# Value products of a head in two groups of three key tiles instead of three groups of two, beside the cluster work of the next pair

## The chip, the core and the metric

The kernel runs on one core of one Trainium2 chip. The metric is the device time of one execution in microseconds (us). The core's engines are TensorE (PE in the profile; PEld is its loading of weights), VectorE (DVE), ScalarE (ACT), GpSimd (POOL) and SyncE (SP), which here only issues DMAs.

## What is computed

The program chains three parts: an attention whose mask joins queries and keys of one cluster, a layer that mixes tokens, and two feed-forward networks. The change lies in the attention, for which the reference is, cut to what matters:

```python
batch, n_heads, seq, head_dim = (2, 8, 768, 64);  n_clusters = 16
q_assign = np.argmax(np.einsum('bhsd,hcd->bhsc', q_n, c_n), axis=-1)     # normalised q, centroids
k_assign = np.argmax(np.einsum('bhsd,hcd->bhsc', k_n, c_n), axis=-1)
mask = q_assign[:, :, :, None] == k_assign[:, :, None, :]
scores = scale * np.matmul(q, k.transpose(0, 1, 3, 2))
scores = np.where(mask, scores, -1000000000.0)
attn = exp(scores - max);  attn = attn / (np.sum(attn, axis=-1, keepdims=True) + 1e-09)
return np.matmul(attn, v).astype(np.float32)
```

Its output, 2 x 768 x 512, goes through h = x @ U @ V over the tokens, added to x, then relu(u @ w_ch1) @ w_ch2 added to u, then a gated network with a convolution over the tokens.

## The kernel before

All work of the attention runs in one loop of steps. There are 16 heads (two batches of eight), taken in eight pairs, and 6 query tiles of 128 rows per head, so 96 steps n; s = n mod 12 is the step in its pair, and r = (n - 7) mod 6 the place in the plan for the value products of head g, which run seven steps behind. The order is written by hand: each engine works through its own row of instructions in the order in which the function step() issues them (a manual schedule), and waits only for data or for a tile to be free.

What step n issues on PE, in this order:

- s_mm(n + 2): the scores of query tile n + 2 against all 768 keys, in four products. L349 (sc<-ab) brings the numbers, L360 (sc<-cd) a second part that also carries, in 16 rows of cd, the one-hot of the cluster, which is the mask. The tile of PSUM (ps_s) that they fill has two copies.
- if the table asks for it, onehot_t (L256): six transposes of the next pair's one-hot; from these ScalarE makes the tile os (onehot_rows, L262), which four DMAs of SP bring into the rows of cd (L270).
- the value products pv_mm (L403) of the key tiles that PLAN names for r: for one key tile k two products side by side, weights v, moving the transposed exponentials of all six query tiles of the head. The result stands in the PSUM tile pv (one copy) over all six key tiles.
- fin_t (L419): three transposes of a head's finished sum, after ScalarE has copied it out (fin_a, L412). Or, in some steps, a product of the token mixing of the batch that is done (L644, L664, L666).
- in step s = 0 sims_wide (L210): similarities to the centroids for the next pair but in the first; in step s = 2 sims_turn (L224), their transposes.
- t_mm(n) (L387): six transposes of the exponentials of step n, in two PSUM tiles of three (tr).

The other engines in step n: ScalarE and VectorE each copy one half of the transposes of step n - 1 out (t_out, L394); ScalarE computes the exponentials of step n + 1 (s_exp, L378); VectorE the row minimum of the negated scores of step n + 2 (s_max, L366). VectorE scales a finished head (fin_x: L425 reciprocals, L428 x<-at) and makes the one-hot of the next pair in five operations, L241 to L249, at the steps of ONEHOT_AT. Small tiles (tr, at, simw, sim, oht, and the mixing's) share three PSUM tiles, ps_t. In odd steps a weight word of later stages is made ready (L456 on ScalarE, L464 and L469 on VectorE).

PLAN has one entry for heads 0 to 14 and one for head 15: a table from r to key tiles, and the r at whose step fin_a follows. ROWS_AT is the step of onehot_t, first for pairs from the second on, then for the first pair. ONEHOT_AT holds the steps of the five operations, likewise.

Of the kernel before, what the change touches and what calls it, by code (L numbers as in the profile page):

```python
# [33 lines left out]
def tile_kernel(ctx: ExitStack, tc: tile.TileContext, qk, vv, cen, u_w, v_w, w1, w2, win, wout, conv, out):  # L34
# [4 lines left out]
    NT = S // P  # L39
# [340 lines left out]
    NK = NT // 2  # L380
# [325 lines left out]
            pump()  # L706


    PLAN = ({2 * k: (2 * k, 2 * k + 1) for k in range(NK)}, NT - 2), ({k: (2 * k, 2 * k + 1) for k in range(NK)}, NK - 1)
    MIX_AT = (2, 4, 8, 10)  # L710

    RAW_AT, V_AT = (5, 8), (8, 10)
    SIM_AT, TURN_AT, ONEHOT_AT, ROWS_AT = 0, (2, 2), ((2, 3, 3, 4, 4), (2, 3, 4, 5, 6)), (6, 7)

    def step(n):
        pair, s = divmod(n, 2 * NT)
# [18 lines left out]
        g, r = divmod(n - NT - 1, NT)  # L735
        ks, last = PLAN[g == NHEAD - 1]
        if 0 <= g < NHEAD:
# [513 lines left out]
```

## Time and profile before

| | |
|---|---|
| device time, median of 3 runs | 648.49 us (648.18 to 649.43) |
| the profiled execution | 649.08 us, of which its span is 647.3 us |
| attention stage | until about 244 us of the span |
| PE busy over the span | 637.2 us, 98% |
| VectorE, ScalarE, GpSimd busy | 430.7 (67%), 368.9 (57%), 304.8 us (47%) |
| TensorE clock granted | full in the whole span |

A busy PE need not be at its peak: products overlap, and what counts is the time from one start to the next. In the timeline below each row gives the start, the length, the engine, the line, what is written from what, the shapes and the number of instructions in a row; in brackets stands the idle time before and who ended it. PE's products of values appear as twice as many instructions as the program writes (x8 for a group of two key tiles).

### The profile page before, as it was taken

How to read it: one execution, taken by the hardware profiler on the slowest of the kernel's cores; microseconds unless marked ns; L12 is line 12 of the kernel's file. 1: busy time of each engine (PE TensorE's matmuls, PEld its weight loads, DVE VectorE, ACT ScalarE, POOL GpSimd, SP SyncE). 2: the span in 40 equal slices, each digit the busy share in tenths (PEclk: the TensorE clock that was granted, in tenths of full speed). 3: DMA queues.
4: the chain of work that ended last, by engine and by line, in shares of the span. 5: the costliest groups of instructions: out<-in, count | busy, mean ns of one | idle time of the engine just before them, and what ended most of it. 6: DMA issues, size and time to landing. Idle time of an engine off the chain costs nothing.

```text
span 647.3 us, 10456 instructions
## 1 busy us (share of the span) xinstructions
PE 637.2 (98%) x3850; PEld 545.7 (84%) x3850; DVE 430.7 (67%) x841; ACT 368.9 (57%) x749; POOL 304.8 (47%) x308
## 2 busy tenths in 40 slices
PE   8999999999999999999999999999999999999997
PEld 5767676666777766999899999999999998889986
DVE  6878787786868785496576666666656468641762
ACT  5867676767767764745554434343354488654730
POOL 3744444256544721913967454554346455413330
PEclk9999999999999999999999999999999999999999
DMA  7495676737353321102333232222212211200022
GB/s 187 102 237 125 130 165 123 169 72 180 64 128 74 91 66 33 34 1 66 104 124 100 66 97 66 66 66 65 66 33 69 95 33 61 71 1 1 1 99 97
DMA packets 17860, 55.50 MB, mean 86 GB/s; under 512 B 3120, under 2 KB 3760, under 8 KB 17808
## 3 DMA queue, kind: packets, MB, share of 16 engines
q1 hardware_dynamic: 14208, 40.08, 21.4%
q0 software_dynamic: 3600, 14.75, 11.5%
q8 instruction: 30, 0.49, 0.3%
q14 instruction: 22, 0.18, 0.1%
HBM read 50.19 MB, written 3.15 MB: 82 GB/s over the span
## 4 chain that ended last, share of the span: by engine, by line
PE 45%; DVE 4%; ACT 3%; POOL 1%; issue 1%; DVEq 0%; POOLq 0%
PE po L970 8%; PE acc L887 6%; PE acc L886 6%; PE acc L888 6%; PE pd L826 4%; PE pb L826 4%; PE pa L826 4%; DVE cv L941 2%; PE g L919 2%; PE g L920 2%; PE g L918 2%; PE pc L826 2%; DVE h L947 1%; ACT cv L937 1%; POOL wl L569 0%
## 5 line engine op out<-in xcount | busy, mean ns | idle before, releaser
L366 DVE TENSOR_SCALAR_CACHE_REDUCE e<-sc 128x768 f32<-128x768 f32 x96 | 91.6, 955 | 14.7 <-PE sc L360 13.2
L890 DVE TENSOR_TENSOR xa<-acc,xa 128x384 f32<-128x384 f32 x128 | 70.1, 554 | 37.4 <-PE acc L888 37.4
L378 ACT ACTIVATE e<-sc,nb 128x768 f32<-128x768 f32 x96 | 87.0, 906 | 7.9 <-DVE e L366 7.4
L886 PE MATMUL acc<-r,vh 128*128 128x384 f32 x256 | 86.3, 337 | 0.1
L887 PE MATMUL acc<-r,vh 128*128 128x384 f32 x256 | 85.7, 335 | 0.3 <-POOL r L869 0.3
L387 PEld LDWEIGHTS tr<-identf,e 128*128 128x128 f32 x576 | 64.6, 140 | 25.2 <-issue 6.8
L888 PE MATMUL acc<-r,vl 128*128 128x384 f32 x256 | 85.6, 334 | 0.0
L387 PE MATMUL tr<-identf,e 128*128 128x128 f32 x576 | 81.7, 277 | 0.3 <-DVE pt L394 0.2
L403 PE MATMUL pv<-pt,rv 128*64 128x384 f32 x384 | 72.6, 499 | 0.0
L394 ACT COPY pt<-tr 128x384 f32<-128x384 f32 x96 | 45.9, 479 | 42.5 <-PE tr L387 42.4
L394 DVE COPY pt<-tr 128x384 f32<-128x384 f32 x96 | 53.2, 554 | 23.4 <-PE tr L387 22.1
L595 POOL TENSOR_TENSOR vl<-wx,vh 128x512 fp32r<-128x512 f32 x24 | 30.8, 1297 | 61.1 <-ACT vh L594 61.1
L349 PE MATMUL sc<-ab 128*128 128x384 f32 x192 | 57.5, 380 | 0.9 <-ACT e L378 0.6
L941 DVE SCALAR_TENSOR_TENSOR cv<-h,cw,cv 128x383 f32<-128x383 f32 (+1 forms) x64 | 38.2, 620 | 25.8 <-ACT cv L937 24.7
L360 PE MATMUL sc<-cd 80*128 80x384 f32 x192 | 49.5, 340 | 0.1
L886 PEld LDWEIGHTS acc<-r,vh 128*128 128x128 f32 x256 | 48.0, 188 | 1.7 <-DVE xa L890 0.8
L887 PEld LDWEIGHTS acc<-r,vh 128*128 128x128 f32 x256 | 48.1, 188 | 0.6 <-POOL r L869 0.6
L888 PEld LDWEIGHTS acc<-r,vl 128*128 128x128 f32 x256 | 48.1, 188 | 0.0
L403 PEld LDWEIGHTS pv<-pt,rv 128*64 128x64 f32 x384 | 23.4, 136 | 28.8 <-issue 28.3
L869 POOL TENSOR_TENSOR r<-q,r 128x384 fp32r<-128x384 f32 x16 | 16.3, 1016 | 58.7 <-ACT r L868 55.2
L469 DVE SCALAR_TENSOR_TENSOR wx<-wb,wy 128x512 int32<-128x512 int32 (+1 forms) x42 | 28.0, 667 | 21.8 <-POOL vl L595 11.0
L569 POOL TENSOR_TENSOR wl<-wx,wh 128x512 fp32r<-128x512 f32 (+1 forms) x32 | 36.4, 1153 | 10.4 <-ACT wh L568 5.2
(241 smaller groups left out, 1527.2 us busy)
## 6 DMA issues: line engine op xcount, KB each, us to landing
raw<-in_w_dram SPq DMA_DIRECT2D x32, 512.0 KB, 3.8
cd<-in_qk_dram POOLq DMA_DIRECT2D x15, 384.0 KB, 4.5
ab<-in_qk_dram POOLq DMA_DIRECT2D x15, 384.0 KB, 5.6
raw<-in_win_dram SPq DMA_DIRECT2D x8, 512.0 KB, 3.8
raw<-in_wout_dram SPq DMA_DIRECT2D x8, 512.0 KB, 3.7
rv<-in_vv_dram SPq DMA_DIRECT2D x8, 384.0 KB, 4.5
out_dram<-xa SPq DMA_DIRECT2D x12, 256.0 KB, 2.0
ab<-in_qk_dram POOLq DMA_DIRECT2D x15, 192.0 KB, 5.8
```

The source lines that it names most:

```text
L349: nc.tensor.matmul(ps[:, f, 0:HS], ab[:, 0, c0:c0 + P], ab[:, 1, f * HS:(f + 1) * HS], start=True, stop=False)
L366: nc.vector.tensor_scalar(out=e, in0=ps[:, :, 0:HS], scalar1=-SCALE, scalar2=3e38, op0=ALU.mult, op1=ALU.min, accum_out=nb,)
L378: nc.scalar.activation(e, ps[:, :, 0:HS], AF.Exp, scale=SCALE, bias=nb, accum_out=st["sum", n // NT][:, n % NT:n % NT + 1])
L387: nc.tensor.transpose(pt[:, k, :], e[:, i, k * P:(k + 1) * P], identf)
L394: (nc.scalar.copy if i == 0 else nc.vector.tensor_copy)(to, st.pop(("t", n, i)))
L403: nc.tensor.matmul(acc[i * D:(i + 1) * D], vts[b, h // 2][:, h % 2, k], pt[:, k, i * NK:(i + 1) * NK].rearrange("p a b -> p (a b)"), start ...
L826: nc.tensor.matmul(o, l[:, k, w], r[:, k], start=first and not more, stop=last, skip_group_check=more)
L886: nc.tensor.matmul(acc, wh[:, f, ds_], r[:, 0], start=f == 0, stop=False)
L887: nc.tensor.matmul(acc, wh[:, f, ds_], r[:, 1], start=False, stop=False)
L888: nc.tensor.matmul(acc, wl[:, f, ds_], r[:, 0], start=False, stop=f == 1)
L890: nc.vector.tensor_add(o, acc, o)
L970: nc.tensor.matmul(po, g[:, ts], w[:, f], start=n == 0, stop=n == 6 * len(cs) - 1)
```

## The change

Three tables change, nothing else:

```diff
-    PLAN = ({2 * k: (2 * k, 2 * k + 1) for k in range(NK)}, NT - 2), ({k: (2 * k, 2 * k + 1) for k in range(NK)}, NK - 1)
+    PLAN = ({2: (0, 1, 2), 5: (3, 4, 5)}, NT - 1), ({k: (2 * k, 2 * k + 1) for k in range(NK)}, NK - 1)
...
-    SIM_AT, TURN_AT, ONEHOT_AT, ROWS_AT = 0, (2, 2), ((2, 3, 3, 4, 4), (2, 3, 4, 5, 6)), (6, 7)
+    SIM_AT, TURN_AT, ONEHOT_AT, ROWS_AT = 0, (2, 2), ((2, 2, 3, 3, 4), (2, 3, 4, 5, 6)), (6, 8)
```

For heads 0 to 14 the value products ran at r = 0, 2 and 4, two key tiles each, which are the odd steps of a pair; now they run at r = 2 and 5, three key tiles each, in steps s = 0, 3, 6 and 9. fin_a follows in the step of the last group (r = 5 instead of 4), and fin_t stays at the next r = 0, one step behind it instead of two. Head 15 keeps its plan. In the pairs from the second on, two of VectorE's five operations of the one-hot go one step ahead (step 3 to 2, 4 to 3); the first pair's transposes of the one-hot go from step 7 to step 8.

On PE, from step 10 of one pair to step 0 of the next (the third and fourth pair), there stands before (of the products L210 one row is shown):

```order
L349 MATMUL sc<-ab 128x384 x2
L360 MATMUL sc<-cd 128x384 x2
L387 MATMUL tr<-identf,e 128x128 x6
L349 MATMUL sc<-ab 128x384 x2
L360 MATMUL sc<-cd 128x384 x2
L403 MATMUL pv<-pt,rv 64x384 x4
L387 MATMUL tr<-identf,e 128x128 x6
L349 MATMUL sc<-ab 128x384 x2
L360 MATMUL sc<-cd 128x384 x2
L210 MATMUL simw<-rq,cbq 32x384
```

and in the changed kernel:

```order
L349 MATMUL sc<-ab 128x384 x2
L360 MATMUL sc<-cd 128x384 x2
L387 MATMUL tr<-identf,e 128x128 x6
L349 MATMUL sc<-ab 128x384 x2
L360 MATMUL sc<-cd 128x384 x2
L387 MATMUL tr<-identf,e 128x128 x6
L349 MATMUL sc<-ab 128x384 x2
L360 MATMUL sc<-cd 128x384 x2
L403 MATMUL pv<-pt,rv 64x384 x6
L210 MATMUL simw<-rq,cbq 32x384
```

The group has moved from step 11 to step 0, grown by two products, and stands directly ahead of the similarities; steps 10 and 11 hold scores and transposes alone. In the same way steps 4 and 5 do, ahead of step 6, where the one-hot's transposes are followed by a group.

On PE at the end of the stage, from the scores of the last query tile to the first product of the next stage (L826), before:

```order
L360 MATMUL sc<-cd 128x384 x2
L403 MATMUL pv<-pt,rv 64x384 x4
L387 MATMUL tr<-identf,e 128x128 x12
L403 MATMUL pv<-pt,rv 64x384 x4
L387 MATMUL tr<-identf,e 128x128 x6
L826 MATMUL pa<-u_2734,wh 128x384
```

and in the changed kernel:

```order
L360 MATMUL sc<-cd 128x384 x2
L403 MATMUL pv<-pt,rv 64x384 x6
L387 MATMUL tr<-identf,e 128x128 x18
L403 MATMUL pv<-pt,rv 64x384 x6
L826 MATMUL pa<-u_2732,wh 128x384
```

The transposes of the last three steps now stand in one row, and the last group of head 14 has moved from between them to behind them.

On ScalarE in the first pair, around the rows made of the one-hot (L262), before:

```order
L378 ACTIVATE e,sum<-sc,nb 128x768
L262 ACTIVATE os<-oht,ohs 64x768
L456 ACTIVATE wb<-raw 128x192
L394 COPY pt<-tr 128x3x128
L378 ACTIVATE e,sum<-sc,nb 128x768
```

and in the changed kernel:

```order
L378 ACTIVATE e,sum<-sc,nb 128x768
L456 ACTIVATE wb<-raw 128x192
L394 COPY pt<-tr 128x3x128
L378 ACTIVATE e,sum<-sc,nb 128x768
L262 ACTIVATE os<-oht,ohs 64x768
```

L262 has moved behind one more copy and one more exponential.

## Rows read from the trace of the kernel before

**Rows 1.** Waits of PE, 60 to 230 us: total us, how often, longest.

```profile
PE tr L387 <- DVE pt L394: 0.2, 1, 0.2
```

**Rows 2.** Timeline of PE, third pair, steps 1 to 5.

```profile
72.42 0.59 PE L349 MATMUL sc<-ab 128*128 128x384 f32 x2
...
77.38 0.59 PE L349 MATMUL sc<-ab 128*128 128x384 f32 x2
...
78.25 1.51 PE L403 MATMUL pv<-pt,rv 128*64 128x384 f32 x8
79.70 0.88 PE L387 MATMUL tr<-identf,e 128*128 128x128 f32 x6
80.33 0.59 PE L349 MATMUL sc<-ab 128*128 128x384 f32 x2
...
81.71 0.62 PE L349 MATMUL sc<-ab 128*128 128x384 f32 x2
```

**Rows 3.** Timeline, all engines: bare steps at the start, then a step at 108.82.

```profile
25.04 0.62 PE L349 MATMUL sc<-ab 128*128 128x384 f32 x2
...
25.80 0.90 ACT L378 ACTIVATE e<-sc,nb 128x768 f32<-128x768 f32 x1 [0.45 <-DVE e L366]
...
26.84 0.61 PE L349 MATMUL sc<-ab 128*128 128x384 f32 x2 [0.17 <-ACT e L378]
...
28.45 0.62 PE L349 MATMUL sc<-ab 128*128 128x384 f32 x2
...
108.82 0.59 PE L349 MATMUL sc<-ab 128*128 128x384 f32 x2
...
110.95 0.90 ACT L378 ACTIVATE e<-sc,nb 128x768 f32<-128x768 f32 x1 [0.34 <-DVE e L366]
```

**Rows 4.** Timeline of PE inside the group of rows 2, two narrow windows.

```profile
78.63 0.81 PE L403 MATMUL pv<-pt,rv 128*64 128x384 f32 x4
...
78.95 0.82 PE L403 MATMUL pv<-pt,rv 128*64 128x384 f32 x4
```

**Rows 5.** Timeline of PE, third pair, step 0.

```profile
70.13 0.59 PE L349 MATMUL sc<-ab 128*128 128x384 f32 x2
...
71.00 0.51 PE L210 MATMUL simw<-rq,cbq 128*32 128x384 f32 x1
...
71.78 0.87 PE L387 MATMUL tr<-identf,e 128*128 128x128 f32 x6
```

**Rows 6.** Timeline of PE, one-hot's transposes: first pair step 7, second pair step 6.

```profile
30.25 0.47 PE L256 MATMUL oht<-identb,oh 128*64 128x128 bf16 x5 [0.83 <-DVE oh L249]
...
32.00 0.88 PE L387 MATMUL tr<-identf,e 128*128 128x128 f32 x6
...
56.20 0.59 PE L349 MATMUL sc<-ab 128*128 128x384 f32 x2
...
58.15 0.59 PE L349 MATMUL sc<-ab 128*128 128x384 f32 x2
```

**Rows 7.** Timeline of VectorE, fourth pair, steps 1 and 2.

```profile
102.86 0.19 DVE L425 RECIPROCAL rs<-sum 128x6 f32<-128x6 f32 x1
103.81 0.56 DVE L428 TENSOR_TENSOR x<-at,rs 128x384 f32<-128x384 f32 x1 [0.77 <-PE at L419]
104.46 0.56 DVE L394 COPY pt<-tr 128x384 f32<-128x384 f32 x1
```

**Rows 8.** First pair: timeline, then DMA issues (KB each, us to landing).

```profile
31.88 2.40 SPq L270 DMA_DIRECT2D cd<-os  x4
...
37.67 0.30 PEld L360 LDWEIGHTS sc<-cd 80*128 80x128 f32 x2 [0.41 <-issue]
...
cd<-os SPq DMA_DIRECT2D x4, 48.0 KB, 4.9
```

**Rows 9.** Timeline at the end of the stage.

```profile
243.09 0.47 ACT L394 COPY pt<-tr 128x384 f32<-128x384 f32 x1
...
244.34 0.59 PE L826 MATMUL pa<-u,wh 128*128 128x384 f32 x2
```

## The prediction

> **What bounds the kernel now.** I read the waits of TensorE (PE) first. In the steady part of the attention stage, 60 to 230 us, PE waits for another engine once, 0.2 us in all [rows 1]: there the stage lasts as long as PE's own row of instructions. So an instruction or a switch of tile that is taken from PE is a gain in full, but only while nobody else becomes late, and the second question is how much room the other engines have. The timeline of PE gives what a step costs, from one first similarity product to the next (a is that moment below). A plain step (scores, six transposes) takes 81.71 - 80.33 = 1.38 us; a step with a group of two key tiles takes 80.33 - 77.38 = 2.95, so such a group costs 1.57 [rows 2]. Two neighbours with such a group, a head's closing transposes (fin_t) and the turn of the similarities take 77.38 - 72.42 = 4.96, so fin_t and the turn cost 4.96 - 2.95 - 1.38 = 0.63, about half each [rows 2].
>
> The room is seen in a loop through three engines. Scores have two PSUM tiles. From a to the exponential that reads the scores is 110.95 - 108.82 = 2.13 (VectorE's row minimum lies between them), and from the start of the exponential to the next scores into the same tile 26.84 - 25.80 = 1.04 [rows 3]. So step n+2 cannot begin sooner than 3.17 us after step n. Two plain steps are 2.76 of PE's work, a plain one and one with a group 4.33. Before the change every second step holds a group, so the loop is never seen after the first group. Ahead of it, in the bare steps at the start, it is: the starts 25.04, 26.84 and 28.45 are 1.80 and 1.61 apart instead of 1.38, and PE waits for the exponential by name [rows 3].
>
> **The change, what it saves.** Heads 0 to 14 get two groups of six products in place of three of four. In the trace a group of two key tiles is eight instructions in four starts of two side by side; the second and third stand at 78.63 and 78.95, so a start is 0.32 and a key tile 0.64 [rows 4]. A group of three tiles then costs 1.57 + 0.64 = 2.21. Per head 3 x 1.57 - 2 x 2.21 = 0.29, over 15 heads **4.35**.
>
> The similarities of the next pair come right behind a group, in six pairs. Alone they cost 72.42 - 70.13 - 1.38 = 0.91 [rows 2, 5]; behind a group they cost the way from the group's last start to their first, X, then 71.78 - 71.00 = 0.78 from their first to the transposes [rows 5], less the way Y from the group's last start to the transposes, which they cut off. Y is 79.70 - 78.95 - 0.32 = 0.43 [rows 2, 4]. X is not in the trace. Its ends are a start inside a group, 0.32, and Y, the way to products that use the array in another cut, as the similarities' do. I take that end, the nearer row: 0.91 - 0.78 = 0.13, times six **0.8** (with X = 0.32, 0.24 and 1.4). The Trainium skill, in TensorEngine Tiling (Array Packing), Key Properties, says that a change of the tiling mode drains the engine; products of values have 64 columns and similarities 32, so by that rule X is at the dear end and the sum stays 0.8; the rows around groups agree with it, none shows this pair.
>
> The one-hot's transposes stand ahead of a group in six pairs. Alone they cost 58.15 - 56.20 - 1.38 = 0.57; ahead of a group they stood once already, in the first pair, where the two took 32.00 - 30.25 = 1.75 to the transposes against 79.70 - 78.25 = 1.45 for a group alone [rows 2, 6]. So 0.27 is saved six times and lost once, since the first pair's now stand apart: **1.35**. Sum of the gains 6.5 us.
>
> **What it costs.** Plain steps now come in twos between the groups: steps 1 and 2, 4 and 5, 7 and 8, 10 and 11 of a pair.
> (1) Steps 4-5 and 10-11 hold nothing else, except where the token mixing fills them, from step 8 of the fifth pair to step 8 of the seventh. That leaves five places at 4-5 and four at 10-11 in which 2.76 us of work meets the loop's 3.17: 9 x 0.4 = **3.6**. The wait stands at the next step's scores, and on PE the group stands behind those: it cannot be worked off meanwhile. The Trainium skill, TensorE: Matmul & The Clock Gate, Part 3, The mechanism, says that products start strictly in program order, only weight loads go ahead; by that rule, too, the group waits, and it speaks against this change; the waiting starts of rows 3 agree.
> (2) Steps 7-8 hold fin_t (2.76 + 0.32 = 3.08 against 3.17): 0.1. Steps 1-2 hold fin_t and the turn (3.39), and here another wait ends last: VectorE, after the minimum of the scores (done by about 2.1 behind a), does the reciprocals, 0.19, the scaled output x that reads fin_t's tile, 0.56, and only then its half of the transposes, 0.56 [rows 7]: 3.4, while PE wants that PSUM tile (there are three) for the second half of the next transposes 3.39 - 0.3 = 3.1 behind a. Between 0 and 0.3, I take 0.2. Before, the group in the step behind gave the cover. Seven places 7-8 with 0.1, six at 1-2 with 0.2 and the last pair (no turn) with 0.1 are 2.0. In three or so of them a weight word on VectorE or the mixing's copy on ScalarE stands ahead of the copy that frees the tile as well, some 0.35 each: **3.0** together (1.0 to 4.5).
> (3) The first pair. Its one-hot's transposes go from step 7 to step 8, and the rows built from them (L262) follow about 1.7 us later, so the four DMAs that bring them to the scores' operand, issued at 31.88, are issued at some 33.6. They took 4.9 us to land, behind loads, and PE waited for them: its weight load waited 0.41 before 37.67 [rows 8]. In the new order PE is there about 0.75 sooner (a group of 1.57 and a wait of 0.83 for the one-hot [rows 6] are gone from step 7, 0.64 and 0.27 are added, and some 0.7 goes to the loop and to the tile that the late rows hold). If the DMAs land when they did, since the loads in front of them set that, PE waits 0.75 more; if they land all of the 1.7 later, 2.4; if they are 0.5 sooner, 0.3. I take 0.75, because the landing time is far over what 48 KB need and the loads are not moved. Steps 10-11 of this pair add 0.35: **1.1** (0.3 to 2.5).
> (4) The end. Before, a group stood between the last transposes but one and the last, and covered the last exponential and ScalarE's copy at 243.09 that frees a PSUM tile for them. That cover moves behind them: the last transposes begin no sooner than 243.09 + 0.47, 243.6, or, if the tile holds up their second half alone, 0.3 sooner; from their start to the next row is 0.63 [rows 2], then comes the group of three tiles, 1.45 + 0.64 from its first product to what follows it [rows 2, 4], and only then the product for the next stage that began at 244.34 [rows 9]: 246.0 to 246.3, 1.7 to 2.0 later. Of this 0.64 is the third key tile, in the sum already, which leaves 1.0 to 1.35: **1.2** (0.6 to 1.4 as bounds).
>
> Sum of the costs 3.6 + 3.0 + 1.1 + 1.2 = 8.9, less 6.5 is +2.4. The profiled execution took 649.08 (span 647.30), which becomes 651.5; it lies 0.6 above the median of the runs, 648.49, so the forecast is 648.49 + 2.4 = **650.9**. The later stages have the same instructions, and nothing moves there.
>
> The parts of the one-hot on VectorE that go one step sooner (two of five) stand in step 2 and 3 instead of 3 and 4. They have the whole step 4 and 5 as cover until the transposes in step 6; I price them at nothing, and at up to 0.3 in step 2, inside (2), where that cover is not the point: the copy behind them is.
>
> **Rivals.** *The waits cancel the gains* (same). The loop may be shorter where the minimum is not behind another operation, say 3.0: then (1) is 9 x 0.25, (2) near 2, and with (3) and (4) the costs are 6.5, the gains' own size: 648 to 649.5. Against it stands 3.17 from two separate rows and the early steps, which are no faster.
> *The groups' switches are the larger thing* (faster). Point from which it decides: the waits in the twos of plain steps are below 0.15 each, since VectorE and ScalarE, which a long group leaves idle, take each minimum and exponential up sooner than in rows 3, and the loop shrinks below 2.9. Then (1) is 1.3, (2) 0.8, (3) and (4) 2.0: 4.1 against 6.5 or 7, 645.6 to 646.5. For it: a step with a group gives the loop 4.33 - 3.17 = 1.2 us of slack to catch up in. Against it: both parts of the loop in rows 3 begin with the engine free, so nothing in them is a queue that could go.
> *A queue builds up* (much slower). ScalarE gets the copy out of the group's tile (L412) and that of the similarities (L215), each as large as the copy of 0.47 in rows 9, in the same step 0, and VectorE the one-hot's parts in step 2; where this ends after the next exponential is due, each of six pairs loses another 0.5 twice: + 6, 655.
> *It does not do what it says:* the order as built shows two groups per head and the similarities and one-hot's transposes beside them, so I leave this no chance of its own.
>
> **How the numbers follow.** Slower by the waits as summed (649.8 to 653) 0.50; a queue beside it, 0.10; cancelled 0.25; faster 0.15. What a measurement of this kernel can tell from no change is about 0.2%, 1.3 us: faster is below 647.2, slower above 649.8. That gives 0.15, 0.25 and 0.60. The range takes the forecast and the cancelling case, the bounds of (2) to (4), and part of the two ends: 646.9 to 653.8. The forecast's own range is 649.3 to 653.
>
> **What would show it.** In the profile after: PE waits for the exponential (L349 <- L378) about nine times 0.4 at starts of steps 0 and 6; transposes wait for VectorE's x or copy in steps 2 and 8; a pair of heads (twelve steps) takes longer, not shorter; groups cost 2.2 over a plain step; PE's busy time falls by about 6 while the span does not. It is wrong if two plain steps in a row take 2.8 us (the loop has room then), if twelve steps become shorter by about 0.8 (the gains of two heads and of the neighbours in full), or if the first product after the attention stage comes sooner than before.

## The result and the profile after

The changed kernel takes 652.71 us (median of 6 runs, 652.08 to 653.09) beside 649.38 of the kernel before on the same chip: a ratio of 1.0051, 95% interval 1.0040 to 1.0061. That is 3.3 us slower, 2.6 to 4.0; 2.4 were forecast, with 646.9 to 653.8 as the range. The profiled execution's span is 650.7 us, 3.4 more than before, so the profile shows the whole of it.

The row of the page with the engines' busy time, changed kernel:

```profile
PE 636.8 (98%) x3850; PEld 549.8 (84%) x3850; DVE 427.2 (66%) x841; ACT 368.3 (57%) x749; POOL 305.5 (47%) x308
```

PE works 0.4 us less than before, over a span 3.4 longer. Its waits in the attention stage, 40 to 250 us (total us, how often, longest):

```profile
PE sc L349 <- ACT e L378: 1.5, 8, 0.2
PE simw L210 <- DMA rk<-in_qk_dram: 0.8, 1, 0.8
PE tr L387 <- ACT pt L394: 0.4, 1, 0.4
PE tr L387 <- ACT e L378: 0.3, 1, 0.3
PE tr L387 <- DVE pt L394: 0.3, 1, 0.3
PE tr L387 <- ACT xa L672: 0.2, 1, 0.2
```

Before, there was the one wait of [rows 1]. These totals understate what is lost: step 5 below is 0.41 longer than a plain step, while the wait at its end has 0.17. The starts tell it. The timeline of PE, third pair, from step 0 on (which answers to [rows 2, 5 and 6]; each row of L349 is the start of a step, those left out among them being step 2 at 76.57 and step 8 at 90.89):

```profile
70.47 0.62 PE L349 MATMUL sc<-ab 128*128 128x384 f32 x2 [0.18 <-ACT e L378]
...
71.38 2.16 PE L403 MATMUL pv<-pt,rv 128*64 128x384 f32 x12
73.46 0.51 PE L210 MATMUL simw<-rq,cbq 128*32 128x384 f32 x1
...
74.25 0.87 PE L387 MATMUL tr<-identf,e 128*128 128x128 f32 x6
74.88 0.59 PE L349 MATMUL sc<-ab 128*128 128x384 f32 x2
...
78.50 0.59 PE L349 MATMUL sc<-ab 128*128 128x384 f32 x2
...
82.10 0.60 PE L349 MATMUL sc<-ab 128*128 128x384 f32 x2
...
83.48 0.61 PE L349 MATMUL sc<-ab 128*128 128x384 f32 x2
...
85.27 0.62 PE L349 MATMUL sc<-ab 128*128 128x384 f32 x2 [0.17 <-ACT e L378]
...
86.18 0.47 PE L256 MATMUL oht<-identb,oh 128*64 128x128 bf16 x5
...
88.57 0.87 PE L387 MATMUL tr<-identf,e 128*128 128x128 f32 x6
89.20 0.59 PE L349 MATMUL sc<-ab 128*128 128x384 f32 x2
...
92.36 0.60 PE L349 MATMUL sc<-ab 128*128 128x384 f32 x2
```

A reader should see three things. The loop: 85.27 - 82.10 = 3.17 us for two bare steps, to the hundredth what [rows 3] gave, and the scores at 85.27 name the exponential; step 5 takes 1.79 instead of 1.38 (step 4, at 1.38, is not longer). The group: step 3 takes 82.10 - 78.50 = 3.60, so a group of three tiles costs 2.22 over a plain step. The neighbours: step 0 is 74.88 - 70.47 = 4.41, step 6 89.20 - 85.27 = 3.93.

In step 2, which takes 78.50 - 76.57 = 1.93 instead of 1.69, VectorE comes last, in the order that the prediction gave: the scaled output x, then its half of the transposes; the second half of PE's next transposes waits for that copy by name, at its weight load:

```profile
77.12 0.56 DVE L428 TENSOR_TENSOR x<-at,rs 128x384 f32<-128x384 f32 x1
...
77.59 0.55 DVE L394 COPY pt<-tr 128x384 f32<-128x384 f32 x1
...
78.19 0.31 PEld L387 LDWEIGHTS tr<-identf,e 128*128 128x128 f32 x3 [0.15 <-DVE pt L394]
```

By stages, from the starts of steps: the first pair and step 12 (from step 0 to step 13) take 2.4 us more than before; the six pairs from there to step 85 take 0.3 less in all (0.13 to 0.18 more in each of the first three, 0.12 to 0.37 less in the three where the token mixing stands); from step 85 to the first product of the next stage 1.2 more; after it nothing. So what is lost lies at the two edges of the stage. The first pair, PE and SP's issues:

```profile
33.38 2.40 SPq L270 DMA_DIRECT2D cd<-os  x4
...
37.00 0.59 SPq L92 DMA_DIRECT2D rk<-in_qk_dram  x1
...
37.55 0.58 PE L360 MATMUL sc<-cd 80*128 80x384 f32 x2 [0.80 <-DMA cd<-os]
...
43.28 0.83 PE L210 MATMUL simw<-rq,cbq 128*32 128x384 f32 x2
44.87 0.48 PE L210 MATMUL simw<-rk,cbk 128*32 128x384 f32 x1 [0.75 <-DMA rk<-in_qk_dram]
```

and the end of the stage, which answers to [rows 9]:

```profile
244.56 0.47 ACT L394 COPY pt<-tr 128x384 f32<-128x384 f32 x1
...
245.08 0.55 PE L387 MATMUL tr<-identf,e 128*128 128x128 f32 x3 [0.39 <-ACT pt L394]
245.56 2.16 PE L403 MATMUL pv<-pt,rv 128*64 128x384 f32 x12
...
247.65 0.61 PE L826 MATMUL pa<-u,wh 128*128 128x384 f32 x2
```

### The profile page after: what moved, and what is told of

The parts are those of the page before. It is cut to its first block, busy times and chain, and to the rows that moved or that the text cites. A ratio compares the mean times of both kernels' runs of the same rounds, so it can differ in the third digit from the quotient of the medians.

```text
span 650.7 us, 10464 instructions
## 1 busy us (share of the span) xinstructions
PE 636.8 (98%) x3850; PEld 549.8 (84%) x3850; DVE 427.2 (66%) x841; ACT 368.3 (57%) x749; POOL 305.5 (47%) x308
## 4 chain that ended last, share of the span: by engine, by line
PE 45%; DVE 4%; ACT 3%; POOL 1%; issue 1%; DVEq 0%; POOLq 0%
PE po L970 8%; PE acc L888 6%; PE acc L886 6%; PE acc L887 6%; PE pd L826 4%; PE pb L826 4%; PE pa L826 4%; DVE cv L941 2%; PE g L919 2%; PE g L920 2%; PE g L918 2%; PE pc L826 2%; DVE h L947 1%; ACT cv L937 1%; POOL wl L569 0%
## 5 line engine op out<-in xcount | busy, mean ns | idle before, releaser
L403 PE MATMUL pv<-pt,rv 128*64 128x384 f32 x384 | 69.5, 494 | 0.0
L349 PE MATMUL sc<-ab 128*128 128x384 f32 x192 | 57.8, 382 | 2.8 <-ACT e L378 2.2
L403 PEld LDWEIGHTS pv<-pt,rv 128*64 128x64 f32 x384 | 26.2, 136 | 28.0 <-issue 25.0
```

The lines of the kernel that those rows point to most:

```text
L349: nc.tensor.matmul(ps[:, f, 0:HS], ab[:, 0, c0:c0 + P], ab[:, 1, f * HS:(f + 1) * HS], start=True, stop=False)
L403: nc.tensor.matmul(acc[i * D:(i + 1) * D], vts[b, h // 2][:, h % 2, k], pt[:, k, i * NK:(i + 1) * NK].rearrange("p a b -> p (a b)"), start ...
```

## The experiments

All ratios are to the kernel before, run beside each on the same chip (its medians 649.35, 649.41 and 649.74 in the three sets; 0.001 is 0.65 us). The changed kernel stands at 1.0051; it was not run again beside these, so a difference to it by the ratios carries both intervals and is uncertain by 1 to 2 us.

**Is PE idle in the bare steps?** e5_dummy adds work there to the changed kernel:

```diff
-            for k in range(NK):
+            for k in [*range(NK if i == 0 and n in (17, 23, 29, 35, 41, 47, 53, 83, 89) else 0), *range(NK)]:
```

> The changed kernel with work added that does nothing: in nine bare steps (steps 5 and 11 of a pair where no mixing stands) the first three transposes are done twice, some 0.33 us of PE each, 3.0 us in all. Theory (PE waits 0.42 us there for the loop anyway): the time rises by less than 0.6 us. Rival (PE's own row sets the time there): it rises by about 3.

Measured: 652.59 us, 1.0052 (1.0031 to 1.0072), as the changed kernel; the rival's 3 us would have been 1.0097. In its timeline step 5 of the third pair holds nine transposes and is as long as with six, 84.98 - 83.19 = 1.79:

```profile
83.19 0.61 PE L349 MATMUL sc<-ab 128*128 128x384 f32 x2
...
83.99 1.15 PE L387 MATMUL tr<-identf,e 128*128 128x128 f32 x9
84.98 0.62 PE L349 MATMUL sc<-ab 128*128 128x384 f32 x2
```

The nine waits are real: some 0.33 us of work goes into each for nothing. That they are the loop's, this run does not show by itself; the name of the wait (the exponential) and the 3.17 us of two steps do.

**Can the waits be filled by moving work?** e4_fill moves fin_t and the one-hot's transposes into bare steps of the changed kernel:

```diff
-    SIM_AT, TURN_AT, ONEHOT_AT, ROWS_AT = 0, (2, 2), ((2, 2, 3, 3, 4), (2, 3, 4, 5, 6)), (6, 8)
+    SIM_AT, TURN_AT, ONEHOT_AT, ROWS_AT = 0, (2, 2), ((2, 2, 3, 3, 4), (2, 3, 4, 5, 6)), (7, 8)
...
-        done = g - 1 if r == 0 else g if g == NHEAD - 1 and r == last + 1 else -1
+        at = 0 if g == NHEAD - 1 or g % H == 0 else 4
+        done = g - 1 if r == at else g if g == NHEAD - 1 and r == last + 1 else -1
...
```

> The changed kernel with its fillers moved into the bare steps: the closing transposes of a head (fin_t) at place 4 (steps 5 and 11) instead of place 0 (steps 1 and 7), but for the last head of each batch; the one-hot's transposes in step 7 instead of 6 from the second pair on. Every two plain steps then hold 0.3 to 0.6 us more than scores and transposes. Theory (score loop of 3.17 us against 2.76 us of work): the waits at steps 6 and 0 fall from 0.42 to about 0.1, those before step 3 and 9 to about 0.1; 6.2 us of waits become 1.5 to 2.0, the one-hot's lost place beside a group costs 1.5: 2.5 to 3.5 us less than the changed kernel, near 649.7. Rival (the waits come from VectorE's and ScalarE's sums of work, not from a loop): they move with the fillers, and the time is within 0.8 us of the changed kernel or above.

A miss: 656.89 us, 1.0129 (1.0100 to 1.0158), 5.1 us above the changed kernel by the ratios, as the rival had it (the waits move with the work). What was moved on PE took its followers with it. In the profiled execution (its span 653.8 us; 655.6 is the shortest time of its set) step 8 is 92.85 - 90.88 = 1.97 us instead of 1.47: the copy that makes the rows, 0.98 on ScalarE, had lain beside a group and now stands ahead of a copy and an exponential for which PE waits.

```profile
90.57 0.98 ACT L262 ACTIVATE os<-oht,ohs 64x768 fp32r<-64x768 bf16 x1
90.88 0.59 PE L349 MATMUL sc<-ab 128*128 128x384 f32 x2
...
91.44 0.46 ACT L394 COPY pt<-tr 128x384 f32<-128x384 f32 x1
...
91.80 0.90 ACT L378 ACTIVATE e<-sc,nb 128x768 f32<-128x768 f32 x1
...
92.85 0.62 PE L349 MATMUL sc<-ab 128*128 128x384 f32 x2 [0.34 <-ACT e L378]
```

fin_t did better: in step 11 it fits in without making the step longer (1.80 with it as without), in step 5 of the second to fourth pairs at a price (1.96 and 1.97 instead of 1.74 to 1.79), while step 2 becomes 0.1 to 0.2 shorter. The loop alone is therefore not the whole story of a bare step: a long group is cover for VectorE and ScalarE as well, and an operation that leaves it meets the loop. Where the other executions of this kernel lost 0.6 to 6 us more than the profiled one is not settled.

**The end.** e3_tail is the changed kernel and gives head 14 alone the old plan:

```diff
+    OLD = ({2 * k: (2 * k, 2 * k + 1) for k in range(NK)}, NT - 2)
...
-        ks, last = PLAN[g == NHEAD - 1]
+        ks, last = OLD if g == NHEAD - 2 else PLAN[g == NHEAD - 1]
```

> The changed kernel, but head 14 alone keeps the old plan of three groups of two key tiles (places 0, 2, 4). Theory (the last group had covered the last exponential and the copy that frees a tile): the first product of the next stage comes 0.8 to 1.2 us sooner than in the changed kernel, net of the 0.29 that its third group costs, and the time falls by as much. Rival (the end is held by what the next stage needs from VectorE and ScalarE): within 0.3 us of the changed kernel.

Measured: 651.32, 1.0021 (1.0010 to 1.0033), 1.9 us less than the changed kernel by the ratios; in the profile the first product of the next stage stands at 246.63 instead of 247.65, 1.0 sooner, and the span is 1.1 shorter. The profile's 1.0 lies inside the 0.8 to 1.2 expected, the ratios' 1.9 above it; the term is confirmed, in size by the profile.

**The first pair.** Three kernels. e2_rows7 is the changed kernel with `ROWS_AT` (6, 7) instead of (6, 8); e6_rows8 the kernel before with (6, 8) instead of (6, 7); e1_raw7 the changed kernel with the raw loads of the first pair in step 7 instead of 8:

```diff
-    RAW_AT, V_AT = (5, 8), (8, 10)
+    RAW_AT, V_AT = (5, 7), (8, 10)
```

> The changed kernel, but in the first pair the one-hot's transposes and rows are back in step 7 (all else as changed). Theory (the first pair's 2.4 us come from the later rows: SP's row of issues is held 1.5 us longer, and the last key load falls behind a load of 384 KB of GpSimd's queue): step 13 starts near 44.3 instead of 46.3, and the time falls by 1.6 to 2.2 us against the changed kernel. Rival (they come from the groups' new places): step 13 starts after 45.5, the time falls by less than 0.8.

> The kernel before, with one number changed: in the first pair the one-hot's transposes and rows in step 8 instead of 7; groups, similarities and the rest as before. Theory (the later rows alone cost the first pair): step 13 starts 1.5 to 2.4 us later than before, since the last key load lands near 44.7 and the similarities of step 12 wait for it, and the whole is slower by as much. Rival (only with the groups' new places does it cost): within 0.5 us of before.

> The changed kernel with one number changed: in the first pair the loads of the raw queries and keys for the third pair are issued in step 7, ahead of the four DMAs of the one-hot's rows, instead of in step 8 behind them. Theory (SP's row of issues is in order, so the rows, which are ready 1.5 us later, hold up the loads behind them): the wait of about 1.2 us at the similarities of step 12 goes, since the last key load lands near 42 instead of 44.7; the time falls by 1.0 to 1.4 us against the changed kernel (652.7 becomes about 651.5). Rival (the DMA engines are full there, whatever the order of issue): the load lands as late, or something else lands later, and the time stays within 0.4 us.

e2_rows7: 650.80, 1.0017 (1.0003 to 1.0030), 2.2 us less than the changed kernel; its similarities of step 12 wait for no load. In its profile steps 0 to 12 take 28.38 us, 1.4 less than in the changed kernel (29.81) and 0.9 more than before (27.45); the rest of the difference in span, 0.7, lies ahead of step 0, where the kernels do not differ. So by this profile the later rows are 1.4 of the 2.4 that the first pair costs, and 0.9 go with the groups' new places in it.

e6_rows8: 655.99, 1.0094 (1.0061 to 1.0128), more than the 1.5 to 2.4 expected: so one number that moves six transposes, a copy and four DMAs of one pair by a step costs more than the whole change. Counted from the start of step 0 (at 15.57 us here, at 16.46 in the changed kernel), PE is at the similarities 1.2 us sooner than in the changed kernel and the key load is there 0.8 later. PE waits 2.7 us for it and then runs at half clock:

```profile
44.82 0.82 PE L210 MATMUL simw<-rk,cbk 128*32 128x384 f32 x1 [2.74 <-DMA rk<-in_qk_dram]
```

The windows of that execution, from 44.5 to 51 us (length, busy us of PE, PEld, DVE, ACT and POOL, then the granted clock, DMA share, GB/s): 

```profile
44.50:46.00 1.50, 1.18 (x6) 0.23 (x6) 0.00 (x0) 0.00 (x0) 1.36 (x1) 0.60 1.16 258
46.00:47.50 1.50, 1.50 (x10) 1.25 (x7) 0.00 (x0) 0.79 (x2) 1.08 (x1) 0.50 1.07 229
47.50:49.00 1.50, 1.50 (x8) 1.13 (x8) 0.69 (x2) 1.06 (x3) 1.09 (x2) 0.76 1.06 260
49.00:51.00 2.00, 2.00 (x16) 1.17 (x13) 1.23 (x4) 0.00 (x0) 0.00 (x0) 1.00 0.64 121
```

This execution, 652.95 us, is the shortest of its set; what the others, up to 658.92, lost beyond it is not shown.

e1_raw7: 655.36, 1.0088 (1.0070 to 1.0106), slower than the changed kernel by 2.4. The wait at the similarities did go, as the theory had it (step 12 takes 4.39 us instead of 5.97). But SP, with nothing to wait for, now issued the raw loads at 21.6, beside GpSimd's loads for the second pair (from 21.52). GpSimd's subtractions on these start at 27.72 and 30.39 instead of 25.97 and 27.88 (the second waits for a load by name, 0.85 us), so its next loads are issued from 32.17 instead of 29.65, directly ahead of the rows' DMAs (33.23). These took 6.0 us to land instead of 3.2, and PE waited for them:

```profile
40.12 0.58 PE L360 MATMUL sc<-cd 80*128 80x384 f32 x2 [3.53 <-DMA cd<-os]
```

So both halves of the question are answered. The late rows cost the first pair because they stand first in SP's row: the last key load was issued at 37.00 instead of 35.79, and came just beside GpSimd's load of 384 KB (issued at 37.57, before at 37.49), where it had been ahead by 1.7 us. The other traces agree: with a lead of 1.70 to 1.94 us (the kernel before, e2_rows7, e8_mended, b1_adj, b2_mid, b4_mid) PE waits for no key load in step 12; with 0.07 to 0.57 (the changed kernel, e3_tail, e4_fill, e5_dummy, e6_rows8, e7_oldhot, b5_first) it waits 0.6 to 2.7 us. And the DMA engines are full there (share 0.80 to 1.25 from 37 to 46 us), so the load cannot be pulled forward to 21.6 either: the rows' DMAs are also what holds it back until its turn. A place between the two was not tried.

**The one-hot's operations.** e7_oldhot is the changed kernel with VectorE's operations in steps 2, 3, 3, 4, 4 as before.

```diff
-    SIM_AT, TURN_AT, ONEHOT_AT, ROWS_AT = 0, (2, 2), ((2, 2, 3, 3, 4), (2, 3, 4, 5, 6)), (6, 8)
+    SIM_AT, TURN_AT, ONEHOT_AT, ROWS_AT = 0, (2, 2), ((2, 3, 3, 4, 4), (2, 3, 4, 5, 6)), (6, 8)
```

> The changed kernel with the old steps for VectorE's one-hot operations (2, 3, 3, 4, 4). Theory (that part of the change is what keeps the one-hot ready in time, since with two operations in step 4 the last one meets GpSimd's subtraction and ends a step late): the one-hot's transposes in step 6 wait 0.4 us in most of the six pairs, and the time rises by 1.5 to 2.4 us against the changed kernel. Rival (priced at nothing in the prediction: steps 4 and 5 are cover enough): within 0.5 us of the changed kernel.

Measured: 655.22, 1.0074 (1.0058 to 1.0089), 1.5 us above the changed kernel by the ratios, 2.4 by the spans. In step 4 of the second pair the last operation, 0.55 us long elsewhere, meets GpSimd and takes 1.90, and the one-hot's transposes wait for the copy behind it:

```profile
55.10 1.83 POOL L119 TENSOR_TENSOR ab<-rk,cd 64x768 fp32r<-64x768 f32 x1 [0.55 <-DMA cd<-in_qk_dram]
...
55.44 1.90 DVE L249 TENSOR_TENSOR oh<-eq,m 128x384 bf16<-128x384 bf16 x1
...
57.27 0.55 DVE L394 COPY pt<-tr 128x384 f32<-128x384 f32 x1
...
57.86 0.44 PE L256 MATMUL oht<-identb,oh 128*64 128x128 bf16 x5 [0.88 <-DVE pt L394]
```

In the changed kernel the same operation of the third pair starts a hundredth of a microsecond ahead of GpSimd's, and it is GpSimd's that becomes longer:

```profile
84.05 0.55 DVE L249 TENSOR_TENSOR oh<-eq,m 128x384 bf16<-128x384 bf16 x1
84.06 2.22 POOL L119 TENSOR_TENSOR ab<-rk,cd 64x768 fp32r<-64x768 f32 x1 [0.24 <-DMA cd<-in_qk_dram]
```

**Both edges mended.** e8_mended joins e2_rows7 and e3_tail.

> The changed kernel with both of its edges mended: the first pair's one-hot in step 7 and head 14 on the old plan. Theory (two terms that lie in different places and add): 1.9 + 1.4 = 3.3 us less than the changed kernel, so that what is left, two groups in the middle of the stage, is worth 0 +- 0.6 us against the kernel before. Rival (the repaired first pair hands its gain on to a later load or wait): less than 2.3 of it appears.

Measured: 649.97, 0.9997 (0.9985 to 1.0009), 3.5 us less than the changed kernel by the ratios: the 3.3 appear, within what the intervals allow. Its profile (650.43 us, among the longer of its set) has 1.5 less in the first pair and 1.1 less at the end, and 1.3 more in the pairs between, nearly all of it in two steps (n = 42 and 50). Two groups instead of three are worth nothing that can be told from zero in the middle of the stage: what they save, the loop takes back.

**A better version.** b1_adj keeps three groups and puts the neighbours beside them:

```diff
-    SIM_AT, TURN_AT, ONEHOT_AT, ROWS_AT = 0, (2, 2), ((2, 3, 3, 4, 4), (2, 3, 4, 5, 6)), (6, 7)
+    SIM_AT, TURN_AT, ONEHOT_AT, ROWS_AT = 1, (3, 2), ((3, 4, 4, 5, 5), (2, 3, 4, 5, 6)), (7, 7)
...
+        if s == SIM_AT and wide:
+            sims_wide(*ahead)
...
-        if s == SIM_AT and wide:
-            sims_wide(*ahead)
...
```

> The kernel before with its three groups per head, but the similarities and the one-hot's transposes put beside a group: similarities in step 1 right behind the group, their turn in step 3, VectorE's five operations in steps 3, 4, 4, 5, 5, the one-hot's transposes in step 7 ahead of the group. Theory (every second step keeps its group, so no two bare steps stand in a row, and a switch less is a gain in full): 6 x (0.09 + 0.25) = 2.0 us less than before. Rival (the rows, one step later, then come late to the scores that need them at step 10, or VectorE's operations fall behind): no gain, or slower by up to 2 us.

655.22, 1.0084 (1.0055 to 1.0113): a miss. In step 7 fin_t follows the one-hot's transposes; the tile that these hold is free only after ScalarE's copy of 0.98 (PE waits up to 0.9 for it), and VectorE's operations, one step later, meet GpSimd's: in the fourth pair a weight word takes 2.31 us and step 7 5.66 instead of 3.28.

b2_mid is the kernel before with two groups only for heads 8 to 11, where the mixing fills the plain steps:

```diff
+    MID = ({2: (0, 1, 2), 5: (3, 4, 5)}, NT - 1)
...
-        ks, last = PLAN[g == NHEAD - 1]
+        ks, last = MID if 8 <= g <= 11 else PLAN[g == NHEAD - 1]
```

b4_mid adds to it the earlier one-hot operations in the two pairs concerned and moves the closing transposes of head 9 to step 11:

```diff
-            for part, at in enumerate(ONEHOT_AT[nxt == 1]):
+            for part, at in enumerate((2, 2, 3, 3, 4) if pair in (5, 6) else ONEHOT_AT[nxt == 1]):
...
-        done = g - 1 if r == 0 else g if g == NHEAD - 1 and r == last + 1 else -1
+        at = 4 if g == 10 else 0
+        done = g - 1 if r == at else g if g == NHEAD - 1 and r == last + 1 else -1
...
```

b5_first adds to that earlier one-hot operations in the first pair:

```diff
-    SIM_AT, TURN_AT, ONEHOT_AT, ROWS_AT = 0, (2, 2), ((2, 3, 3, 4, 4), (2, 3, 4, 5, 6)), (6, 7)
+    SIM_AT, TURN_AT, ONEHOT_AT, ROWS_AT = 0, (2, 2), ((2, 3, 3, 4, 4), (2, 3, 3, 4, 5)), (6, 7)
```

> The kernel before, with two groups of three key tiles for heads 8 to 11 alone, where the token mixing stands in the plain steps (similarities and one-hot stay in steps 0 and 6). Theory (two groups gain where something fills the plain steps): 4 x 0.29 for the groups and 2 x 0.34 for the neighbours, less 0.6 to 1.0 of waits before steps 3 and 9: 0.8 to 1.3 us less than before. Rival (the waits eat it there too): within 0.3 us of before.

> The kernel before, with two groups for heads 8 to 11 alone, in the two pairs concerned the one-hot's operations in steps 2, 2, 3, 3, 4, and the closing transposes of head 9 four steps later, where no x has to be read ahead of the mixing's transposes. Theory (gains where the mixing fills the plain steps, once the one-hot's wait of 0.4 us at its transposes and 0.46 at step 8 of the sixth pair are gone): 1.0 to 1.4 us less than the kernel before. Rival (the waits move): within 0.4 us of before.

> As the run before it in this set, and in the first pair the one-hot's five operations in steps 2, 3, 3, 4, 5 instead of 2 to 6. Theory (the wait of 0.83 us for the one-hot in step 7 goes, and the rows that are then issued earlier land earlier): another 0.6 to 0.9 us less. Rival (the landing of the rows is set by the loads in front, so PE waits there instead): within 0.3 us of that run.

b2_mid: 650.08, 1.0005 (0.9991 to 1.0020), no difference; its two steps 6 with a group of three last 4.33 us instead of the changed kernel's 3.92, since with the old operations the one-hot comes late there too. b4_mid: 648.26, 0.9979 (0.9965 to 0.9992): 1.4 us faster than the kernel before and 4.7 faster than the changed one, in the direction and of the size expected. It is the only one here that beats both, by little. Its profiled execution (649.96, among the longer of its set; 647.16 to 650.90) shows one thing that can make the times spread: in the third pair, whose code is that of the kernel before, the one-hot's last operation fell behind GpSimd by four hundredths and the transposes two steps later wait 0.92 us:

```profile
82.28 1.81 POOL L119 TENSOR_TENSOR ab<-rk,cd 64x768 fp32r<-64x768 f32 x1 [0.77 <-DMA cd<-in_qk_dram]
82.32 2.18 DVE L249 TENSOR_TENSOR oh<-eq,m 128x384 bf16<-128x384 bf16 x1
...
86.93 0.55 PE L387 MATMUL tr<-identf,e 128*128 128x128 f32 x3 [0.92 <-DVE pt L394]
```

Step 6 of the third pair takes 3.09 us there and that of the fourth 3.32, against 1.95 and 1.96 in the profiled executions of the kernel before and of b5_first, with the same code in both pairs.

b5_first: 649.96, 0.9997 (0.9983 to 1.0010), 1.2 us more than b4_mid by the ratios: neither forecast, and the opposite of the theory. The one-hot's last operation, a step earlier than before, now meets GpSimd's second subtraction:

```profile
27.40 1.81 POOL L120 TENSOR_TENSOR ab<-rk,ab 64x768 fp32r<-64x768 f32 x1
27.44 2.19 DVE L249 TENSOR_TENSOR oh<-eq,m 128x384 bf16<-128x384 bf16 x1
...
30.15 0.44 PE L256 MATMUL oht<-identb,oh 128*64 128x128 bf16 x5 [0.57 <-DVE pt L394]
```

The wait in step 7 is 0.57 us instead of 0.83, for the copy behind that operation; the minimum and the exponential behind it are late as well, and so are the rows, issued 16.9 us after the start of step 0 instead of 15.4 before. PE then waits for the key load in step 12 as in the changed kernel (0.8 us). Besides, VectorE stands in the loop of the bare steps 5 and 6, which became 0.4 and 0.2 us longer.

## Why the prediction was right, and where not

The forecast, slower by 2.4 us through waits that outweigh the switches saved, held in sign and mechanism, and the 3.3 us measured lie inside its range. That the total came out within 1 us is in part luck: one term was 1.4 too small, the gains 0.4 too large, and another term 0.6 too large the other way. Its steps, one by one:

- *The gains.* A group of three tiles was put at 2.21 and takes 2.22. The similarities behind a group cost 4.41 - 1.38 - 2.22 = 0.81, forecast 0.78, and the one-hot's transposes 3.93 - 1.38 - 2.22 = 0.33, forecast 0.30: the way from values to similarities is a little longer than the dearer end that was taken, and the two together save 0.34 a pair instead of 0.40. Sum 6.1 instead of 6.5.
- *(1), the bare steps.* The steps 5 and 11 in the nine places last 1.74 to 1.86 instead of 1.38, 3.8 us in all; forecast 3.6. e5_dummy shows that it is PE's idle time. By name the waits for the exponential are 8, about as many as forecast, but with 1.5 us in all.
- *(2), steps 1-2 and 7-8.* Steps 8 take 1.47 where nothing else stands (0.09 more, forecast 0.1), steps 2 1.93 to 1.94 (0.24 more, forecast 0.2), through VectorE's x and copy as forecast. With the places beside the mixing and 0.16 in step 7 of the last pair the sum is 2.4 instead of 3.0. The extra 0.35 in three places was too much.
- *(3), the first pair: the step that failed.* 2.5 us instead of 1.1, at the upper end of its bounds (the 2.4 of the stages, and 0.1 that the groups and similarities save there). The part that was worked out was right: the rows, issued 1.5 us later, landed when they had before, and PE waited for them (0.80 at 37.55; that it had waited for them before is read from the time, since the row of 0.41 in [rows 8] names no releaser). What was left out is who stands behind them in SP's row: the raw loads of the third pair, whose last part is needed by the similarities in step 12. The first of these start at 43.28, those on the key load only at 44.87, and step 12 takes 5.97 us instead of the 4.4 of later pairs; e2_rows7, without the later rows, has no such wait and 4.41. The prediction named this queue's DMAs, but only the four that were moved.
- *(4), the end.* 1.2 forecast; from step 85 to the first product of the next stage 1.24 more, plus the 0.59 that the two heads' groups save there, less 0.67 of waits in steps 86, 89 and 91 that belong to (1) and (2): 1.2. e3_tail gives 1.0 back net of its third group, as it should.
- *The one-hot's operations, priced at nothing.* In the changed kernel nothing is seen of them, so the price held. What the prediction did not see is what they are for: without this part of the change 1.5 to 2.4 us more are lost (e7_oldhot), by a meeting of two engines that it did not think of.
- *The sum.* 3.8, 2.4, 2.5 and 1.2 less 6.1 is 3.8, beside 3.4 between the spans.
- *A sign that did not come.* PE's busy time was to fall by about 6 us and fell by 0.4. The groups did save their starts, but the profile counts most of the waiting as busy (0.41 us lost in step 5, 0.17 of it as a wait), so busy time could not show it.

The rivals: gains cancelled by waits are what the middle of the stage shows (e8_mended, 0.9997), though not for the reason given there, a shorter loop; it is the edges that decide the sign. No queue built up: the pairs in the middle differ from before by 0.4 us at most, where the rival had 1 us for each.

## What to carry to other kernels

When one engine is full, ask for every pair of its steps whether the other engines' loop (here scores, minimum, exponential, 3.17 us for two steps) still fits without the work that is moved: larger groups save switches, but smaller ones, spread evenly, were the cover. Where a DMA that waits for data is issued later, price every issue behind it in the same row, and who needs that first. And price the edges of a stage apart: here the two edges cost 2.4 and 1.2 us, and the repeated middle nothing.

## What was not expected of the hardware

VectorE and GpSimd keep each other out in some operations. VectorE's operation on two tiles of SBUF (L249, 0.55 us) takes 1.90, 2.18 and 2.19 when GpSimd's subtraction (L119 or L120, 1.8 us) started 0.34, 0.04 and 0.04 us before it (e7_oldhot, b4_mid, b5_first), and GpSimd's takes 2.22 when VectorE was first by 0.01; the copies and minima that VectorE reads from PSUM keep their 0.55 and 0.95 beside the same operations (in the changed kernel at 84.52 and 84.99). The Trainium skill, SBUF — State Buffer, SBUF: two separate sides, says that a pair of ports is shared by the two (on VectorE's side by operations with two inputs in SBUF, among others) and is held by whoever starts first for its whole instruction; the rows agree. Which of the two is first depends here on hundredths of a microsecond and on when a DMA lands (GpSimd's subtraction waits for one by its row), so the same pair of heads loses 1 us in one profiled execution and none in another (b4_mid beside the kernel before).

A wait of 2.74 us on PE in e6_rows8 was followed by about 3 us at half the granted clock, 1.2 instead of 2.4 GHz (0.50 from 46.0 to 47.5, 1.00 again from 49.0), and so was the one of 3.53 us in e1_raw7 (0.50 from 41 to 44); after the wait of 0.75 us at the same place in the changed kernel, where step 12 is 1.6 us longer than in later pairs, the clock stayed at 1.00. An estimate from these windows: 3 us at half the clock lose up to 1.5 us, so each of the two long waits may have cost up to half as much again.
